# A Hyena and expert kernel: forward transform folded onto quarters of the array, with sends, stores and loads placed anew

## The chip, the core and the metric

The kernel runs on one core of one Trainium2 chip. The metric is the device time of one execution in microseconds (us). Names of engines: PE is TensorE's matmul, PEld its loading of weights, DVE VectorE, ACT ScalarE, POOL GpSimd, SP SyncE, which here only issues DMAs.

## The reference

The input is 4 batches of 11456 positions with 128 channels. The first half is a gated long convolution over each batch, by a filter that a small network and a window make; the second routes each of the 45824 rows to one of 8 experts.

```python
u = x * v
Uf, Hf = rfft(u, n=2*S, axis=1), rfft(h_filt, n=2*S, axis=0)
y = irfft(Uf * Hf, n=2*S, axis=1)[:, :S, :]
x = (x * y).reshape(B*S, D)
logits = x @ w_gate + modality_bias[modality_id]
e = argmax(logits); gate = softmax(logits)[e]
out[row] = gate * (relu(x[row] @ w1[e]) @ w2[e])
```

## The kernel before

**The convolution** is done as a transform in two factors (90 by 64) with matmuls in float32. It has, for each batch, an outer part and a middle part. The outer part goes over 16 steps q, each 8 channels: SP loads tiles of u and v (L446), DVE multiplies them (`product`, L451), and PE transforms the product (`forward`, L463; s in rows of the trace) with 64 matmuls of 128 rows by 90 columns that write halves of PSUM's partitions, two at a time; ACT copies the results into A (L466). The middle part goes over 23 groups g: ring loads of the filter's spectrum and two tables (h L579, b L576, c L584, into `rings`), a transform (pz, L595), the multiplication by the spectrum on DVE and POOL (L607 to L619), the transform back (pw, L638).

**The outer stage** from batch 1 on holds two things at once: the forward part of batch b, and the inverse part and routing of batch b - 1. In each step the inverse part turns two pieces of A (wt, L661), ACT copies them (L662), PE transforms them (py, L670), and y is made of the two halves of py: ACT copies one half (L673), DVE adds it to the other (L674) and subtracts it (L675), and multiplies the result by x, loaded at L655, into a row tile xo (L676). Two steps make a pair, of which the routing is done once: a turn of xo (xT, L705), the logits (pl, L716), their turn (lt, L725), the choice of expert (`shift`, `biased`, `choice`: L732 to L767, with an exponential on ACT, L753), the count of rows for each expert (pr, pn, L783 to L794, `send`). The rows go to memory (`store`, L774), and their places in the list of the chosen expert too (`places`, L801). The last outer stage has the inverse part and routing of batch 3 alone.

**Sends.** POOL scatters the rows to their expert's place (L268, one indirect DMA of 128 rows each) from tiles that are read back (L252). `send_rows(n)` puts n of them at a place in POOL's order. An outer step before has four: two behind the product, one behind y's sum, one behind the product with x. In the middle groups one or two follow `L619` from g = 5 on, and the experts issue one every third turn.

**The order** of the work is written by hand. Tables such as `OUTER` give each piece a step offset (`forward:2` is done for q in step q + 2), and within a step the order of the table stands; each engine takes its instructions in that order. `overlapped` and `early` mix the end of one stage with the start of the next by OV, EA, EM steps. Buffers named "a" (11 of 1024 float32 a partition) served x, u, v, y and the middle's parts in turn.

**The experts** take tiles of 512 or 256 rows. For a tile the rows are loaded (x, L991), turned (px, L1052) and split into two float32r parts (L1055, L1056), the weights too (w1r and w2r, L1006 and L1007; wl, L1041); PE forms the hidden layer (ph, L1069 to L1071) and the output (po, L1092 to L1094), which is scattered (L1111). `finale` holds the last pieces of routing, done beside the first tiles.

## Time and profile before

| | us |
|---|---|
| median of 3 runs | 2235.19 |
| lowest and highest | 2232.07, 2238.38 |
| profiled execution | 2249.8 |
| its span | 2248.0 |
| filter, then forward part of batch 0 | 0 to about 150 |
| outer stages of batches 1, 2, 3 | about 260 to 400, 515 to 655, 770 to 910 |
| middle stages of batches 1, 2 | about 400 to 513, 655 to 765 |
| last outer stage | about 1020 to 1115 |
| experts | about 1126 to 2248 |

How to read it: the profile's times are from one execution, recorded in the profiler. A row of a timeline or chain begins with its start in us from the start of the span, then its length in us. "L463" is line 463 of the kernel before. A bracket at the end tells how long the engine had been idle and what ended that.

### The profile page before, as it was taken

To read this page: it belongs to the slowest core of one execution; us is meant where nothing else is said; L and a number is where in the kernel's file an instruction comes from. 1 tells how busy PE (TensorE), PEld (TensorE's weight loads), DVE (VectorE), ACT (ScalarE), POOL (GpSimd) and SP (SyncE) were. 2 spreads that over 40 slices of the span, in tenths; PEclk is the share of its full clock that TensorE was granted. 3 is DMA by queue.
4 is the path that set the end of the run, shared out by engine and by line. 5 is a ranking of instruction groups with operands and counts; after the bars stand their busy time and mean duration, and the time that the engine had idled before them with its cause. 6 is when DMAs were issued, how large, how long until landed. Compare 5 with 4: busy or idle time off the path is not lost.

```text
span 2248.0 us, 49882 instructions
## 1 busy us (share of the span) xinstructions
PE 2160.9 (96%) x18746; PEld 1735.5 (77%) x18746; DVE 1668.0 (74%) x2847; ACT 1225.8 (55%) x2253; POOL 1025.1 (46%) x1032
## 2 busy tenths in 40 slices
PE   8989999899989999899799999999999999999996
PEld 8878777687768767676477888878888888888896
DVE  2348677995779767896877777767778877777796
ACT  4632366226642366225565666656666666666685
POOL 0116300695448754694335555545554333333332
PEclk9999999999999999999999999999999999999998
DMA  9576676777878788774657222222222111111111
GB/s 310 231 269 225 222 225 195 253 254 269 280 245 268 265 274 272 249 252 153 193 179 256 76 73 78 69 64 80 80 72 74 48 47 44 43 48 45 40 42 29
DMA packets 162526, 359.21 MB, mean 160 GB/s; under 512 B 25769, under 2 KB 59389, under 8 KB 162281
## 3 DMA queue, kind: packets, MB, share of 16 engines
q1 hardware_dynamic: 135625, 296.58, 41.0%
q0 software_dynamic: 26496, 59.36, 7.7%
q8 instruction: 150, 2.46, 0.4%
q14 instruction: 95, 0.78, 0.1%
q10 hardware_dynamic: 160, 0.03, 0.0%
HBM read 271.44 MB, written 84.83 MB: 158 GB/s over the span
## 4 chain that ended last, share of the span: by engine, by line
PE 55%; issue 26%; POOL 10%; DVE 4%; DMA 2%; ACT 2%; POOLq 0%; SPq 0%; ACTq 0%; DVEq 0%
PE pw L638 8%; PE s L463 7%; POOL out L1111 6%; PE pz L595 6%; PE py L670 5%; PE wt L661 5%; POOL xs L268 3%; PE po L1094 2%; PE xT L705 2%; PE ph L1069 2%; PE po L1092 2%; PE ph L1070 2%; PE ph L1071 2%; PE po L1093 2%; PE pl L716 1%
## 5 line engine op out<-in xcount | busy, mean ns | idle before, releaser
L1075 DVE SCALAR_TENSOR_TENSOR hl<-ph,hh 128x512 fp32r<-128x512 f32 x724 | 495.4, 689 | 220.8 <-ACT hh L1074 119.7
L1074 ACT ACTIVATE hh<-ph 128x512 fp32r<-128x512 f32 x724 | 433.7, 601 | 343.9 <-PE ph L1071 241.7
L1111 POOL DMA_INDIRECT out<-ot,idx x362 | 360.0, 994 | 556.1 <-DVE ot L1108 463.2
L268 POOL DMA_INDIRECT xs<-back,to x360 | 369.3, 1026 | 289.3 <-DVE y L674 103.8
L1069 PE MATMUL ph<-xh,wh 128*128 128x512 f32 (+1 forms) x792 | 306.3, 387 | 1.3 <-ACT xh L1055 1.3
L1092 PE MATMUL po<-hh,wh 128*128 128x512 f32 (+1 forms) x792 | 298.6, 377 | 4.0 <-issue 2.3
L1094 PE MATMUL po<-hl,wh 128*128 128x512 f32 (+1 forms) x792 | 297.1, 375 | 0.9 <-DVE hl L1075 0.7
L1070 PE MATMUL ph<-xh,wl 128*128 128x512 f32 (+1 forms) x792 | 297.1, 375 | 0.0
L1071 PE MATMUL ph<-xl,wh 128*128 128x512 f32 (+1 forms) x792 | 295.4, 373 | 0.0
L1093 PE MATMUL po<-hh,wl 128*128 128x512 f32 (+1 forms) x792 | 295.3, 373 | 0.0
L642 ACT COPY A<-pw 128x512 f32<-128x512 f32 (+1 forms) x184 | 97.7, 579 | 349.2 <-PE pw L638 339.9
L614 DVE TENSOR_TENSOR part<-pz,rings 128x1024 f32<-128x1024 f32 (+1 forms) x184 | 211.4, 1190 | 2.8 <-POOL part L619 2.8
L638 PEld LDWEIGHTS pw<-rings,part 64*128 64x128 f32 x2880 | 177.3, 189 | 35.6 <-issue 27.2
L638 PE MATMUL pw<-rings,part 64*128 64x128 f32 x2880 | 202.2, 279 | 1.7 <-POOL part L619 1.7
L595 PE MATMUL pz<-A,rings 128*64 128x256 f32 x1440 | 177.3, 388 | 13.8 <-DVE part L614 6.0
L609 POOL TENSOR_TENSOR more<-more 128x256 f32<-128x256 f32 (+1 forms) x92 | 73.9, 803 | 236.8 <-issue 150.0
L463 PE MATMUL s<-fwd,seq 128*64 128x90 f32 x4096 | 171.3, 242 | 9.5 <-issue 5.3
L1092 PEld LDWEIGHTS po<-hh,wh 128*128 128x128 f32 x792 | 149.2, 188 | 36.7 <-issue 4.4
L1094 PEld LDWEIGHTS po<-hl,wh 128*128 128x128 f32 x792 | 149.4, 189 | 35.5 <-DVE hl L1075 5.4
L463 PEld LDWEIGHTS s<-fwd,seq 128*64 128x64 f32 x4096 | 161.8, 137 | 18.6 <-issue 6.8
L1071 PEld LDWEIGHTS ph<-xl,wh 128*128 128x128 f32 x792 | 149.4, 189 | 29.7 <-DVE xl L1056 0.4
L1093 PEld LDWEIGHTS po<-hh,wl 128*128 128x128 f32 x792 | 149.3, 188 | 26.2
(184 smaller groups left out, 3705.2 us busy)
## 6 DMA issues: line engine op xcount, KB each, us to landing
rings<-hs SPq DMA_DIRECT2D x88, 512.0 KB
seq<-in_u SPq DMA_DIRECT2D x64, 512.0 KB
seq<-in_v SPq DMA_DIRECT2D x64, 512.0 KB
seq<-in_x SPq DMA_DIRECT2D x64, 512.0 KB
xr<-xo SPq DMA_DIRECT2D x64, 365.6 KB
back<-xr SPq DMA_DIRECT2D x72, 325.0 KB
rings<-in_c_b SPq DMA_DIRECT2D x88, 256.0 KB
rings<-in_c_c SPq DMA_DIRECT2D x88, 256.0 KB
```

What stands on the lines that cost most here:

```text
L268: s = pool.indirect_dma_start(out=xs, out_offset=bass.IndirectOffsetOnAxis(ap=ix, axis=0), in_=src, in_offset=None, bounds_check=E * R - 1 ...
L463: pe.matmul(v[64 * c:64 * c + 64, blk, j], u[:, blk, 4 * h + j], fwd[:, c], start=True, stop=True)
L638: pe.matmul(pw[par][:, to:to + D], t[at], k["c"][at, q, c], start=i == 0, stop=i == len(terms) - 1)
L1069: pe.matmul(p, k[0, "h"][:, f:f + D], k["xh"], start=True, stop=False)
L1070: pe.matmul(p, k[0, "l"][:, f:f + D], k["xh"], start=False, stop=False)
L1071: pe.matmul(p, k[0, "h"][:, f:f + D], k["xl"], start=False, stop=True)
L1074: act.activation(hh, ph, AF.Relu)
L1075: dve.scalar_tensor_tensor(hl, ph, 0.0, hh.bitcast(F32), op0=ALU.max, op1=ALU.subtract)
L1092: pe.matmul(po, k[1, "h"][:, f], hh[:, t], start=g == 0, stop=False)
L1093: pe.matmul(po, k[1, "l"][:, f], hh[:, t], start=False, stop=False)
L1094: pe.matmul(po, k[1, "h"][:, f], hl[:, t], start=False, stop=g == NCH - 1)
L1111: s = pool.indirect_dma_start(out=out, out_offset=bass.IndirectOffsetOnAxis(ap=k["idx"][:, j:j + 1], axis=0), in_=ot[:, j, :], in_offset=N ...
```

## The change

Forward parts of batches 1 to 3 are folded. The host reverses the order of one half of u and v, and the two halves of the product then come as a sum and a difference. DVE multiplies into a new tile p (109 partitions), POOL subtracts its halves and DVE adds them, into two slots of the ring `around`; the transform then has matmuls of at most 64 rows, in the order of four quarters (rows of the upper or lower half, columns of the left or right one). The number of matmuls is the same. Batch 0 keeps the old form.

y: ACT copies both halves of py (1024 elements) and DVE makes sum and difference of that copy a step later, in `combine`. Sends: one behind the product is gone, and the counts are 1 or 2 behind y's sum (turn about), 1 behind the product with x, 2.5 a step on the mean; in the middle stages they follow from the first group on for batches 2 and 3, and from g = 6 for batch 1; three every eight turns in the experts. Fetching rows back now goes by how many sends are left (`ready`). Stores come a step later; store and places of a batch's last step are issued in groups of the middle stage. The loads of x, u and v turn in 7 rows of `around`, p and y in 2 tiles, the middle's parts in 9. The ring's places differ, OV, EA and EM too. In the experts the results are three turns behind, in place of two, and the first tile's rows are loaded between w1r and w2r.

```diff
-OUTER = ("turn0:1 turn1:1 lturn:3 biased:3 forward:2 load_x:0 product:1 half:2 choice:3 "
-         "inverse:1 logits:2 send:4 shift:2 load:0 store:4 places:5")
-LAST = ("lturn:5 biased:5 send:6 turn0:1 choice:5 turn1:1 inverse:2 logits:4 half:3 shift:4 load_x:0 store:5 places:6")
+OUTER = ("turn0:1 turn1:1 biased:5 choice:5 send:6 forward:2 power:5 combine:2 gate:5 product:1 logits:4 half:3 "
+         "inverse:1 lturn:4 shift:4 load_x:0 load:0 store:6 places:6")
+LAST = ("lturn:5 biased:5 send:6 turn0:1 choice:5 power:5 gate:5 turn1:1 inverse:2 combine:2 logits:4 half:3 shift:4 "
+        "load_x:0 store:5")
...
-FIRST = "forward:17 load:0 product:16"
+FIRST = "forward:17 product:16 load:13"
...
-OV, EA, EM = 2, 3, 4
+OV, EA, EM = 4, 2, 5
...
-NA, NXO = 11, 3
+NA, NU, NS, NXO = 9, 7, 2, 3
...
-        for _ in range(min(n, len(waiting))):
+        for _ in range(n):
+            if ready and len(waiting) <= 2 * RC:
+                fetch(ready.pop(0))
+            if not waiting:
+                return
...
+        def next_a():
+
+            at = counts["around"] = (counts.get("around", -1) + 1) % NA
+            return around[:, at]
+
+        def rows_of(src, n=NU):
+
+            at = counts["rows", n] = (counts.get(("rows", n), -1) + 1) % n
+            t = around[:, at]
+            sp.dma_start(t, src)
+            return t
...
-            ("h", 2 * GW, (8 * GW, 0, 2 * GW)),
-            ("b", GW, (10 * GW, 4 * GW, 5 * GW)),
-            ("c", GW, (11 * GW, 6 * GW, 7 * GW)))}
+            ("h", 2 * GW, (8 * GW, 0, 4 * GW)),
+            ("b", GW, (10 * GW, 2 * GW, 6 * GW)),
+            ("c", GW, (11 * GW, 3 * GW, 7 * GW)))}
...
                 for name in ("u", "v"):
-                    t = kept[q, name] = new_a("seq")
-                    sp.dma_start(t, a[name][b, q])
+                    kept[q, name] = rows_of(a[name][b, q], NU if b else NA)
             def product(q):
-                u = kept[q, "u"]
-                s = dve.tensor_mul(u, u, kept.pop((q, "v")))
-                paced(s, 2)
+                if b == 0:
+                    of = kept[q, "of"] = kept.pop((q, "u"))
+                    dve.tensor_mul(of, of, kept.pop((q, "v")))
+                    return
+                u, v = kept.pop((q, "u"))[0:PU], kept.pop((q, "v"))[0:PU]
+                p, of = new_a("p")[0:PU], around[:, NU + q % (NA - NU)]
+                dve.tensor_mul(p, u, v)
+                pool.tensor_sub(of[0:PU, 512:1024], p[:, 0:512], p[:, 512:1024])
+                dve.tensor_add(of[0:PU, 0:512], p[:, 0:512], p[:, 512:1024])
+                kept[q, "of"] = of
             def transform(q):
-                u = kept.pop((q, "u")).rearrange("p (b d n) -> p b d n", b=2, n=N2)
+                of = kept.pop((q, "of")).rearrange("p (c d n) -> p c d n", c=2, n=N2)
+                whole = [(c, blk, slice(0, D), blk) for blk in range(2) for c in range(2)]
+                parts = [(c, blk, slice(64 * blk, 64 * blk + HALF), c)
+                         for c, blk in ((0, 0), (1, 1), (1, 0), (0, 1))]
                 for h in range(2):
                     p = pair("s1")
                     v = p[:, :, 0:4 * N1].rearrange("p b (d k) -> p b d k", d=4)
                     for j in range(4):
-                        for blk in range(2):
-                            for c in range(2):
-                                pe.matmul(v[64 * c:64 * c + 64, blk, j], u[:, blk, 4 * h + j],
-                                          fwd[:, c], start=True, stop=True)
+                        for c, blk, at, of_c in parts if b else whole:
+                            pe.matmul(v[64 * c:64 * c + 64, blk, j], of[at, of_c, 4 * h + j],
+                                      fwd[at, c], start=True, stop=True)
...
+                at = 3 * ((g + 1) % 3)
+                part = [around[:, at + i, 0:n * 4 * D].rearrange("p (c q b d) -> p c q b d", c=2, b=2, d=D)
+                        for i in range(2)]
+                more = around[:, at + 2, 0:n * 4 * D].rearrange("p (i c q d) -> p i c q d", i=2, c=2, d=D)
...
-                if g == 4 and b > 0:
-                    fetch(b - 1)
+                if g == 5 and b > 0:
+                    ready.append(b - 1)
...
-                if g > 4:
+                if g > 5 or b > 1:
...
-                t = kept[q] = new_a("seq")
-                sp.dma_start(t, a["x"][b, q])
+                if q == 0:
+                    counts.pop(("rows", NU), None)
+                kept[q] = rows_of(a["x"][b, q])
...
-                y = new_a("y")
-                act.copy(y[:, 512:1024], py[:, 1])
-                paced(dve.tensor_add(y[:, 0:512], py[:, 0], y[:, 512:1024]))
-                dve.tensor_sub(y[:, 512:1024], py[:, 0], y[:, 512:1024])
-                paced(dve.tensor_mul(xo_of(b, q // 2)[:, :, q % 2, :, 0:D], four(y),
-                                     four(kept.pop(q))))
-
-            return load, turn, transform
+                y = kept[q, "y"] = new_a("y")
+                act.copy(y, py.rearrange("p c m -> p (c m)"))
+
+            def combine(q):
+
+                y = kept.pop((q, "y"))
+                paced(dve.tensor_add(y[:, 0:512], y[:, 0:512], y[:, 512:1024]),
+                      1 + (q % 3 > 0 if b == nb - 1 else q % 2))
+                dve.scalar_tensor_tensor(y[:, 512:1024], y[:, 512:1024], -2.0, y[:, 0:512],
+                                         op0=ALU.mult, op1=ALU.add)
+                paced(dve.tensor_mul(xo_of(b, q // 2)[0:PU, :, q % 2, :, 0:D], four(y[0:PU]),
+                                     four(kept.pop(q)[0:PU])))
...
-                ex = powers[0:PU]
-                act.activation(ex[:, 0:E], dl, AF.Exp)
...
+            def power(o):
+                act.activation(powers[0:PU, 0:E], kept.pop(("dl", o)), AF.Exp)
+
+            def gate(o):
+                xo = xo_of(b, o)
                 se = rt.tile([PU, NC], F32, tag="se", name="se")
-                dve.tensor_reduce(se, ec(ex), axis=AX.X, op=ALU.add)
+                dve.tensor_reduce(se, ec(powers[0:PU]), axis=AX.X, op=ALU.add)
...
+                later.append([lambda f=todo[n]: f(NQ - 1) for n in ("store", "places")])
+                todo["store"] = but_last(todo["store"], 2)
+                todo.pop("places")
...
+                for k, g in enumerate(later.pop() if b else ()):
+                    mid[5 + k] = lambda f=mid[5 + k], g=g: (f(), g())
...
+    swap = lambda a: np.stack([a[0], a[1, :, ::-1]])
+    chan8 = lambda a: swap(a.reshape(2, 64, 2, N2, NQ, 8)).transpose(4, 0, 1, 2, 5, 3).reshape(NQ, D, -1)
```

In the experts:

```diff
-                sp.dma_start(k["w", 0], a["moe_w1"][ds(e, 1)].rearrange("e p f -> p (e f)"))
-                sp.dma_start(k["w", 1], a["moe_w2"][ds(e, 1)].rearrange("e (c p) d -> p (e c) d", p=D))
+                first = [lambda: sp.dma_start(k["w", 0], a["moe_w1"][ds(e, 1)].rearrange("e p f -> p (e f)")),
+                         lambda: sp.dma_start(k["w", 1], a["moe_w2"][ds(e, 1)].rearrange("e (c p) d -> p (e c) d", p=D))]
+                return first
+
+            of = raw_weights() if i < NDYN else []
+            for part in of[:1] + [rows] + of[1:] if i == 0 else [rows] + of:
+                part()
...
-            if lo == 0 and at >= FL + len(finale) + 2 and len(waiting) <= 2 * RC and not fetched:
-                fetched.append(fetch(nb - 1))
-            if lo == 0 and at % 3 == 0:
+            if lo == 0 and at == FL + len(finale) + 2:
+                ready.append(nb - 1)
+            if lo == 0 and 3 * at % 8 < 3:
...
-            result(at - 2)
-            if c == (5 if i <= last and tiles[i][2] == T else 2):
+            result(at - 3)
+            whole = i <= last and tiles[i][2] == T
+            if c == (4 if whole else 2):
                 rows_turn(i + 1)
+            if c == (5 if whole else 3):
                 rows_out(i - 1)
```

On DVE, these are the rows of an outer step from y's sums on, before (score, ix, lg, base are the routing's; seq holds u and v):

```order
L674 TENSOR_TENSOR y<-py,y 128x512
L675 TENSOR_TENSOR y<-py,y 128x512
L676 TENSOR_TENSOR xo_84<-y,seq 128x2x4x128
L790 TENSOR_TENSOR score<-pr,base 109x128
L791 TENSOR_TENSOR base<-base,pn 128x8
L792 TENSOR_TENSOR score<-score,oh_96 109x128
L794 TENSOR_REDUCE ix<-score 109x2x8
L732 TENSOR_TENSOR lg<-wf,bias 109x128
L732 TENSOR_TENSOR score<-wf,bias 109x128
L734 TENSOR_TENSOR lg<-lg,score 109x128
L741 TENSOR_TENSOR lg<-lt,lg 109x128
L451 TENSOR_TENSOR seq<-seq 128x1024
```

and after (around holds x, u, v and the folded product):

```order
L830 TENSOR_TENSOR score<-pr,base 109x128
L831 TENSOR_TENSOR base<-base,pn 128x8
L832 TENSOR_TENSOR score<-score,oh_95 109x128
L834 TENSOR_REDUCE ix<-score 109x2x8
L709 TENSOR_TENSOR y<-y 128x512
L711 SCALAR_TENSOR_TENSOR y<-y 128x512
L713 TENSOR_TENSOR xo_86<-y,around 109x2x4x128
L476 TENSOR_TENSOR p<-around 109x1024
L478 TENSOR_TENSOR around<-p 109x512
L769 TENSOR_TENSOR lg<-wf,bias 109x128
L769 TENSOR_TENSOR score<-wf,bias 109x128
L771 TENSOR_TENSOR lg<-lg,score 109x128
```

y's sums stand behind the row counts, both read y alone, and the product has the addition of its halves behind it.

On SP, where the outer stage of batch 1 ends and its middle stage begins (xr the stored rows, xi the places, rings the middle's loads), before:

```order
L774 DMA xr_58<-xo_85 90x1x1040 x2
L801 DMA xi_62<-ix 45x128 x2
L584 DMA rings<-in_c_c 128x512
L576 DMA rings<-in_c_b 128x512
L579 DMA rings<-hs 128x1024
```

and after:

```order
L814 DMA xr_58<-xo_84 90x1x1040 x2
L613 DMA rings<-in_c_c 128x512
L605 DMA rings<-in_c_b 128x512
L608 DMA rings<-hs 128x1024
...
L814 DMA xr_58<-xo_85 90x1x1040 x2
L613 DMA rings<-in_c_c 128x512
L605 DMA rings<-in_c_b 128x512
L608 DMA rings<-hs 128x1024
L841 DMA xi_62<-ix 45x128 x2
```

The last store and the places stood ahead of these ring loads, and now come behind three and four groups of them.

On SP, from the end of the last outer stage to the experts' first loads, before (TENSOR_LOAD reads a tile's expert and start):

```order
L774 DMA xr_61<-xo_86 90x1x1040 x2
L252 DMA back_92<-xr_60 128x650
L984 TENSOR_LOAD tab_100
L1002 TENSOR_LOAD tab_100
L1006 ISA
L1006 DMA w1r<-in_moe_w 128x1024
L1007 ISA
L1007 DMA w2r<-in_moe_w 128x8x128
L991 ISA
L991 DMA x<-xs 128x520
```

and after:

```order
L253 DMA back_92<-xr_60 128x650
L386 DMA around<-in_x 128x1024
L253 DMA back_90<-xr_60 128x650
L1034 TENSOR_LOAD tab_100
L1053 TENSOR_LOAD tab_100
L1057 ISA
L1057 DMA w1r<-in_moe_w 128x1024
L1042 ISA
L1042 DMA x<-xs 128x520
L1058 ISA
L1058 DMA w2r<-in_moe_w 128x8x128
```

The store is gone from there, and x stands between the two loads of weights.

## Rows read from the trace of the kernel before

**Rows 1.** The page's first part: busy time, share of the span, instructions of each engine.

```profile
PE 2160.9 (96%) x18746; PEld 1735.5 (77%) x18746; DVE 1668.0 (74%) x2847; ACT 1225.8 (55%) x2253; POOL 1025.1 (46%) x1032
```

**Rows 2.** Windows: stretch, length, busy PE, PEld, DVE, ACT, POOL, clock, DMA share, GB/s.

```profile
304.15:321.37 17.22, 17.01 (x210) 12.12 (x208) 12.10 (x26) 11.13 (x20) 0.00 (x0) 1.00 0.71 218
417.12:436.15 19.03, 19.01 (x256) 15.39 (x256) 18.66 (x23) 4.82 (x10) 14.94 (x15) 1.00 0.93 321
1800.00:2000.00 200.00, 200.00 (x938) 164.96 (x937) 154.26 (x252) 131.28 (x236) 67.33 (x68) 1.00 0.16 46
```

**Rows 3.** Chain of waits, outer stage of batch 1 and middle: start, length, instructions.

```profile
301.59 2.63 PE s L463 x64
304.22 0.90 PE xT L705 x8
305.12 1.87 PE py L670 x8
306.98 1.94 PE wt L661 x16
...
314.31 0.87 PE pl L716 x8
...
417.12 2.89 PE pw L638 x48
...
513.37 1.44 PE pw L638 x20
```

**Rows 4.** Timeline of DVE: start, length, instruction, idle before it.

```profile
306.12 0.40 DVE L764 TENSOR_REDUCE se<-powers 109x16 f32<-109x144 f32 x1 [0.17 <-ACT powers L753]
307.67 0.69 DVE L674 TENSOR_TENSOR y<-py,y 128x512 f32<-128x512 f32 x1 [0.83 <-ACT y L673]
310.26 1.22 DVE L451 TENSOR_TENSOR seq<-seq 128x1024 f32<-128x1024 f32 x1
314.98 0.69 DVE L674 TENSOR_TENSOR y<-py,y 128x512 f32<-128x512 f32 x1 [3.50 <-ACT y L673]
1122.43 0.29 DVE L734 TENSOR_TENSOR bs_late<-bs_late,score 109x128 f32<-109x128 f32 x1
```

**Rows 5.** Timelines of DVE and POOL in middle stages, where both work at once.

```profile
206.75 0.69 DVE L618 TENSOR_TENSOR part<-part 128x512 f32<-128x512 f32 x1
206.86 1.71 POOL L619 TENSOR_TENSOR part<-part 128x512 f32<-128x512 f32 x1 [0.84 <-DVE part L614]
741.79 1.27 DVE L618 TENSOR_TENSOR part<-part 128x512 f32<-128x512 f32 x1
741.76 0.74 POOL L609 TENSOR_TENSOR more<-more 128x256 f32<-128x256 f32 x1
743.61 1.27 POOL L619 TENSOR_TENSOR part<-part 128x512 f32<-128x512 f32 x1
```

**Rows 6.** Groups by line: count, busy, mean ns of one, idle before.

```profile
L673 ACT COPY y<-py 128x512 f32<-128x512 f32 x64 | 37.9, 592 | 61.3 <-PE py L670 49.2 <-issue 12.2
L268 POOL DMA_INDIRECT xs<-back,to x360 | 369.3, 1026 | 289.3 <-DVE y L674 103.8 <-issue 67.8 <-DVE mx L749 28.7
```

**Rows 7.** Timeline of PE: waits at the ends of stages.

```profile
415.17 1.95 PE L595 MATMUL pz<-A,rings 128*64 128x256 f32 x16 [2.02 <-DMA rings<-in_c_b]
1087.89 1.13 PE L661 MATMUL wt<-ident,A 128*90 128x128 f32 x8 [0.48 <-ACT rings L710]
1126.33 1.08 PE L1052 MATMUL px<-ident,x 128*128 128x128 f32 x4 [10.79 <-DMA x<-xs]
```

**Rows 8.** DMA issues on SP: start, length, transfer.

```profile
304.26 0.33 SPq L446 DMA_DIRECT2D seq<-in_u  x1
410.69 0.80 SPq L801 DMA_DIRECT2D xi<-ix  x2
412.05 0.37 SPq L576 DMA_DIRECT2D rings<-in_c_b  x1
1118.33 0.80 SPq L991 DMA_DIRECT2D x<-xs  x1
```

83 lines of the change are left out of this document (47 added, 36 removed).

## Prediction

> **What bounds the kernel now.** I read the views in the order in which a stage shows its limit: busy shares, windows by stage, the chain of waits inside one stage, then the timelines of the engines that wait. PE is busy for 96% of the span [rows 1]; that share is an average over unlike stages. The windows [rows 2] split it. In the outer stages, which run the inverse transform and routing of one batch beside the forward transform of the next, one pair of steps takes 17.22 us: PE is busy 17.01, DVE 12.10, ACT 11.13, DMA 71%. In the middle stages (four groups in 19.03 us) PE and DVE are both full, 19.01 and 18.66. In the experts PE is busy for all of 200 us. So PE is the limit nearly everywhere, and only in the outer stages has the next engine much room.
>
> The chain there [rows 3] is PE alone: the forward transform takes 2.63 us a step, the two turns 1.94, the inverse 1.87, the turn to the router 0.90 and once a pair the logits 0.87. DVE waits 3.50 and 0.83 us in the pair for ACT's copy, which waits for PE, and 0.17 more for the exponential [rows 4]. Its own work with issue gaps is so 17.22 - 4.50 = 12.72 us. That is what the change can reach: 3 outer stages (batches 1 to 3 forward) of 8 pairs, 24 pairs in all. Batch 0's forward part and the last outer stage have no folded transform.
>
> **The change part by part. PE.** Folding lets each matmul of the forward transform sum over 45 rows, inside a quarter of 64, where it summed over 128; the number of matmuls (64 a step) and their 90 columns stay, but four can stand in different quarters of the array, where two stood in its halves. The row on the forward transform gives 2.63/64/90 = 0.457 ns a column with two side by side; the logits put four side by side and take 0.87/8/436 = 0.25 ns [rows 3]. At 0.25 ns a step's 64 x 90 columns cost 1.44 us. A second floor is the loading of weights, one load of 64 columns before each matmul: 48 loads of 128 columns are hidden in 2.88 us [rows 3], 60 ns each, so a load of 64 columns needs at most 30 ns, and 64 of them 1.92 us. I keep 1.44 to 1.92 and, as the far end, the old 2.63. PE's pair falls from 17.01 by 2 x 0.71 to 1.19: 14.6 to 15.6 us.
>
> **DVE.** The product stays (1.22 us, row L451 of [rows 4]); the addition of its halves is new, 512 elements wide as the sum of y is, 0.69 us [rows 4]. y's two sums stay and read a copy from SBUF instead of PSUM; I take the same 0.69. So 12.72 + 2 x 0.69 = 14.1 us a pair. Then there is POOL's new subtraction, at the same moment as DVE's addition, since both wait for the product. An addition of this size took 0.69 us when it had begun before POOL's, and POOL's then took 1.71 instead of 1.27; it took 1.27 when it began inside POOL's subtraction [rows 5]. DVE lost 0.58 us there, and POOL 0.44 in the other order. Price per step: 0 at best; at worst what is left of POOL's operation after DVE's addition has ended, 206.86 + 1.71 - 207.44 = 1.13 us. I take 0.58, the one stretch of DVE shown: 2 x 0.58 = 1.2, DVE 15.3 us a pair (14.1 to 16.4).
>
> These prices rest on a rule too. The Trainium skill, "SBUF — State Buffer", section "Who interferes with whom", states that a VectorE operation with two inputs in SBUF and a GpSimd operation that reads SBUF share one port under an exclusive lock, and that the later one blocks fully. The rows agree: 741.76 + 0.74 + 0.69 = 743.19 us, and the addition ended at 743.06. It speaks against this change, for y's two sums now have both inputs in SBUF as well, where one came from PSUM; it is a rival below.
>
> **ACT, POOL, DMA.** ACT copies 1024 elements of y where it copied 512 (0.592 us [rows 6]), at most 0.59 more a step: 11.13 + 1.2 = 12.3 a pair, covered. POOL has 5 sends of 1.026 us a pair [rows 6] where it had 8, and two subtractions of 1.27 to 1.71: under 9 us, covered. The same bytes move in less time: 218 GB/s x 17.22/15.5 = 242, while a middle stage held 321 GB/s without a PE wait [rows 2]; covered.
>
> **The pair.** DVE at 15.3 and PE at 14.6 to 15.6 are close, and before the pair stood 0.21 above its PE (17.22 against 17.01). I add that to 15.3: 15.5 us. The outer term is 24 x (17.22 - 15.5) = -41 us.
>
> **The way into the middle stages.** PE waits 2.02 us for a ring load [rows 7], issued on SP at 412.05 behind the list of places (410.69, which waits for the routing) [rows 8]. The change issues that list after the loads, and starts the middle stage's transforms one turn earlier. The bounds are the whole of the PE wait plus as much again for the earlier start, -4, and 0; I take -3, three times: -9.
>
> **Sends in the middle stages.** Two of them get sends in five more groups, seven each, and one loses a group with sends. Four early groups, mostly without sends, take 19.03 us, 4.76 each [rows 2]; the 19 groups between the two chain rows at 417.12 and 513.37, most with sends, take 96.25/19 = 5.07 [rows 3]. 9 x 0.31 = +2.8; I take +3 (0 to +7, the latter with half of the 14 sends of 1.026 us on the path).
>
> **Last outer stage.** The wider copy of y stands on ACT ahead of the router's copies, for which PE waits 0.48 us [rows 7]. 16 steps x 0.59 = 9.4 if none is covered, 0 if all; half, +5.
>
> **Start of the experts.** PE waits 10.79 us for the first rows [rows 7], issued on SP at 1118.33 [rows 8] behind both weight loads and a store. The change puts them ahead of the second weights and takes the store away. But DVE's routing runs to 1122.72 [rows 4], and SP still waits for a transfer back. Bounds: the whole wait, -11, and +3 for three more pieces of routing behind the turn of the stages; I take -4. **Steady experts:** results three turns behind can't help a PE busy for 200.00 of 200 us: -1 (0 to -4). **Batch 0 and the filter:** later first loads, 0 (-2 to +5).
>
> The sum is -41 - 9 + 3 + 5 - 4 - 1 = -47. The profiled execution took 2249.8 us (span 2248.0), 15 above the median of 2235.19; the terms are differences, so I take them from the median: 2188.
>
> **The rivals.** (1) POOL's subtraction collides with nothing: DVE 14.1, PE 14.6 to 15.6. By PE's lower end the pair is 14.8, the outer term 24 x 2.4 = -58, the time 2171. For it: DVE's addition has no other engine's signal to wait for and starts first, as at 206.75 [rows 5]. (2) The full lock: every subtraction stops the next DVE operation for 1.13 us, DVE 16.4, the pair 16.6, the outer term -15, the time 2214. For it: y's sums and the routing's products now read SBUF twice. (3) The change doesn't do what it says: quarters in one row of the array share a path, the transform stays at 2.63, PE at 17.01. The outer term is 0 and the time 2229. Against it: the logits' 0.25 ns, though these share their rows and only differ in columns, which is why the case stays open.
>
> (4) **Slower: the loop of the loads.** Eleven buffers served x, u, v and y; now x, u and v turn in seven rows. In steady state the load of u waits for the row that y's last product (L713) has just read, and the product of the step after needs it. From L713 over the landing T, then that product and its sum (1.22 + 0.69), half of the routing's small work (12.10 less two steps of 1.22 + 0.69 + 0.69 + 1.22, halved: 2.2, some 2.6 with gaps) and the next y (0.69 + 0.69 + 1.22) to L713 two steps on: the pair is T + 7.1 us. It decides above T = 8.4 and loses from T = 10.1 on. The issue at 304.26 us served a product at 310.26, so T was at most 6.0 [rows 4, 8]; but sends and returning rows are added in two of the three stages. At T = 12 there the pair is 19.1: 16 x 1.9 = +30, the first stage -14, the rest -6: +10, 2245.
>
> The Trainium skill, "TensorE: Matmul & The Clock Gate", section "Wait — 56ns, not 53.3ns?", puts the start-to-start time of matmuls at no less than about 25 ns however small they are. The traced forward transform's 41 ns (2.63/64) neither confirms nor breaks it. By it a step's 64 matmuls would take 1.6 us, an estimate from that page, and rival 1 would come out at 2179 instead of 2171.
>
> **How the numbers follow.** My forecast with the collision of 0.58 us: 0.45 (its own range 2172 to 2204, from the pair at 15.1 to 15.9 and half of the small terms' bounds). Rival 1: 0.18. Rival 2: 0.17. Rival 3: 0.10. Rival 4: 0.10. The predicted time is the likeliest's, **2188**. The range reaches down past rival 1 with the outer-to-middle gain and the experts' start at better values, 2148, and up past rival 3, 2231; about 0.08 is left out below and 0.08 above. A measurement of this kernel can tell about 0.3% from no change, 6.7 us: 2228.5 to 2241.9. Faster: 0.45 + 0.18 + 0.17 and 0.04 of rival 3 = 0.84. The same: 0.05 of rival 3 and 0.03 of rival 4 = 0.08. Slower: 0.01 and 0.07 = 0.08.
>
> **What would show it.** In the profile after: the forward transform's row on the chain at 1.44 to 1.92 us (2.63: rival 3); the pair of steps in the second outer stage at 15.5 us, DVE busy above 90% of it and PE with waits for DVE; the new additions and y's first sum near 0.69 us where POOL is idle and near 1.27 where it subtracts (0.69 throughout: rival 1; DVE idle or stretched by over 1 us a step: rival 2); no wait of the product for a load (waits of over 2 us: rival 4). The PE wait for the ring load at the end of each outer stage should go, and the one for the first rows shrink by some 4 us. My prediction is wrong if DVE's idle time stays, that is if something other than PE's work ended its waits.

## The result and the profile after

The changed kernel takes 2253.28 us (median of 4 runs, 2249.24 to 2255.25), the kernel before 2234.28 (4 runs): a ratio of 1.0085, 95% interval 1.0072 to 1.0098. It is slower by 19 us where 2188 was forecast, and lies above the range.

The page of the changed kernel, its first part, answers [rows 1]:

```profile
span 2247.5 us, 49786 instructions
...
PE 2111.3 (94%) x18746; PEld 1690.8 (75%) x18746; DVE 1769.2 (79%) x2895; ACT 1249.4 (56%) x2253; POOL 1146.0 (51%) x1080
```

PE has 50 us less to do and DVE 101 more. The spans hardly differ, but the profiled execution of before was 15 us above its median. So stages are compared here, not spans.

Windows of the changed kernel: two pairs of outer steps of batch 1, then the end of that stage (the columns are those of [rows 2]).

```profile
315.73:331.98 16.25, 14.64 (x208) 9.70 (x208) 15.13 (x28) 11.52 (x20) 3.43 (x2) 1.00 0.70 240
331.98:349.64 17.66, 15.98 (x207) 10.74 (x207) 15.01 (x28) 11.51 (x20) 3.42 (x2) 0.90 0.64 220
400.00:412.00 12.00, 2.85 (x15) 1.64 (x17) 10.73 (x22) 1.38 (x3) 5.84 (x6) 0.66 0.56 189
```

PE's work in a pair fell as forecast, to 14.64 us, and DVE's rose to 15.1, but the pair takes 16.25 to 17.66 us, not 15.5. In the third window PE is idle for some 9 of 12 us.

PE's timeline there, with the forward transform of an earlier step first (answers [rows 3] and [rows 7]):

```profile
272.24 1.47 PE L492 MATMUL s<-fwd,around 45*64 45x90 f32 x64
273.64 0.96 PE L742 MATMUL xT<-ident,xo 109*128 109x109 f32 x8
...
397.04 2.95 PE L668 MATMUL pw<-rings,around 64*128 64x128 f32 x48
408.95 0.27 PE L823 MATMUL pr<-oh,both 109*128 109x128 bf16 x1 [8.96 <-DVE oh L794]
409.62 3.68 PE L624 MATMUL pz<-A,rings 128*64 128x256 f32 x16
...
725.47 3.68 PE L624 MATMUL pz<-A,rings 128*64 128x256 f32 x16 [5.78 <-DMA rings<-in_c_b]
729.08 4.06 PE L668 MATMUL pw<-rings,around 64*128 64x128 f32 x48
...
1131.92 0.63 PE L1114 MATMUL px<-ident,x 128*128 128x128 f32 x4 [1.39 <-DMA x<-xs]
```

and DVE's, ahead of the row count at 408.95 (L644 belongs to a middle group, L778 begins the choice):

```profile
403.48 2.34 DVE L644 TENSOR_TENSOR around<-pz,rings 128x1024 f32<-128x1024 f32 x2
...
406.47 0.28 DVE L778 TENSOR_TENSOR lg<-lt,lg 109x128 f32<-109x128 f32 x1
```

The transform takes 1.47 us for 2.63. The wait for the first rows of the experts fell from 10.79 us [rows 7] to 1.39. But the row count (pr) of an outer stage's last routing waits 8.96 us for DVE, and so in all three batches (8.96, 9.09, 9.09), where [rows 7] had 2.02 us for a ring load. In the middle stage of batch 2 there is a wait of 5.78 us, and the transform behind it takes 4.06 us for 2.95: the granted clock was at half there.

DVE and POOL in the two steps of a pair (answers [rows 5]), then DVE and PE in the experts' stage:

```profile
550.67 0.89 DVE L832 TENSOR_TENSOR score<-score,oh 109x128 f32<-109x128 f32 x1
...
555.77 0.73 DVE L478 TENSOR_TENSOR around<-p 109x512 f32<-109x512 f32 x1
556.43 1.85 DVE L769 TENSOR_TENSOR lg<-wf,bias 109x128 f32<-109x128 f32 x1
558.20 0.28 DVE L769 TENSOR_TENSOR score<-wf,bias 109x128 f32<-109x128 f32 x1
...
549.71 1.70 POOL L477 TENSOR_TENSOR around<-p 109x512 f32<-109x512 f32 x1 [0.67 <-PE wt L692]
...
555.78 0.98 POOL L273 DMA_INDIRECT xs<-back,to  x1 [0.30 <-DVE p L476]
556.77 1.36 POOL L477 TENSOR_TENSOR around<-p 109x512 f32<-109x512 f32 x1
...
1761.86 0.16 DVE L292 TENSOR_SCALAR fd<-nall 1x8 int32<-1x8 f32 x1 [10.99 <-SPq L989]
...
1763.69 0.79 PE L1154 MATMUL po<-hl,wh 128*128 128x512 f32 x1 [7.35 <-DVE hl L1135]
...
1768.55 0.63 PE L1153 MATMUL po<-hh,wl 128*128 128x512 f32 x1
...
1769.50 0.40 PE L1130 MATMUL ph<-xh,wl 128*128 128x512 f32 x1
```

The routing's first product (L769) lasts as long as POOL's subtraction goes on, 1.85 us for 0.28; in the other step L832 takes 0.89 for 0.28. In the experts DVE stands idle for 10.99 us ahead of a division of eight numbers, which waits for SP; PE waits 7.35 us behind it, and its matmuls run at the lower clock until 1769.1.

Measured from the first turn of one batch to that of the next, the three cycles took 253.3, 254.7 and 254.1 us before and 251.5, 265.3 and 253.0 after; from the last stage's first turn to the experts 102.0 and 101.8. Up to the experts, then, the loss stands in the cycle of batch 2 (10.6 us more); the other two gained 1 to 2 us, where the forecast's outer term alone is some 14 a cycle. Over all these, from the first turn to the experts, the granted clock was at its lower level (0.5) for 13 us before (9 of them in the wait just ahead of the experts) and for 85 after; a second trace of the changed kernel has 72.

### The profile page after: what moved, and what is told of

It reads as the page before. It is cut to its first block, busy times and chain, and to the rows that moved or that the text cites. A ratio compares the mean times of both kernels' runs of the same rounds, so it can differ in the third digit from the quotient of the medians.

```text
span 2247.5 us, 49786 instructions
## 1 busy us (share of the span) xinstructions
PE 2111.3 (94%) x18746; PEld 1690.8 (75%) x18746; DVE 1769.2 (79%) x2895; ACT 1249.4 (56%) x2253; POOL 1146.0 (51%) x1080
## 4 chain that ended last, share of the span: by engine, by line
PE 56%; issue 19%; DVE 9%; DMA 7%; POOL 6%; SPq 1%; ACT 1%; POOLq 0%; DVEq 0%; ACTq 0%
PE pw L668 10%; PE pz L624 7%; POOL out L1171 5%; PE ph L1131 4%; PE ph L1129 4%; PE ph L1130 4%; PE po L1152 4%; PE po L1154 4%; PE po L1153 4%; PE wt L692 3%; PE s L492 3%; PE py L701 3%; DMA xr<-xo 2%; DVE xo L713 2%; PE xT L742 1%
## 5 line engine op out<-in xcount | busy, mean ns | idle before, releaser
L1171 POOL DMA_INDIRECT out<-ot,idx x362 | 379.2, 1047 | 467.0 <-DVE ot L1168 382.4
L273 POOL DMA_INDIRECT xs<-back,to x360 | 398.8, 1108 | 264.6 <-DVE y L709 97.2
L1129 PE MATMUL ph<-xh,wh 128*128 128x512 f32 (+1 forms) x792 | 312.1, 394 | 0.7 <-ACT xh L1115 0.7
L668 PEld LDWEIGHTS pw<-rings,around 64*128 64x128 f32 x4320 | 250.5, 189 | 37.0 <-issue 30.3
L668 PE MATMUL pw<-rings,around 64*128 64x128 f32 x4320 | 267.3, 278 | 2.5 <-POOL around L649 2.4
L644 DVE TENSOR_TENSOR around<-pz,rings 128x1024 f32<-128x1024 f32 (+1 forms) x184 | 211.3, 1189 | 0.0
L624 PE MATMUL pz<-A,rings 128*64 128x256 f32 x1440 | 182.0, 397 | 8.6 <-DMA rings<-in_c_b 5.8
L1130 PEld LDWEIGHTS ph<-xh,wl 128*128 128x128 f32 x792 | 150.7, 190 | 24.5 <-DVE wl L1094 4.6
L1129 PEld LDWEIGHTS ph<-xh,wh 128*128 128x128 f32 x792 | 150.2, 190 | 20.5 <-ACT xh L1115 0.9
L492 PE MATMUL s<-fwd,around 45*64 45x90 f32 (+1 forms) x4096 | 127.7, 254 | 29.9 <-POOL around L477 12.3
```

The source lines that it names most:

```text
L273: s = pool.indirect_dma_start(out=xs, out_offset=bass.IndirectOffsetOnAxis(ap=ix, axis=0), in_=src, in_offset=None, bounds_check=E * R - 1 ...
L624: pe.matmul(pz[at, q, 2 * D * c:2 * D * c + 2 * D], k["b"][:, 2 * q + par, 64 * c:64 * c + 64], A[:, G * g + 2 * q + par].rearrange("p b d ...
L668: pe.matmul(pw[par][:, to:to + D], t[at], k["c"][at, q, c], start=i == 0, stop=i == len(terms) - 1)
L1129: pe.matmul(p, k[0, "h"][:, f:f + D], k["xh"], start=True, stop=False)
L1130: pe.matmul(p, k[0, "l"][:, f:f + D], k["xh"], start=False, stop=False)
L1171: s = pool.indirect_dma_start(out=out, out_offset=bass.IndirectOffsetOnAxis(ap=k["idx"][:, j:j + 1], axis=0), in_=ot[:, j, :], in_offset=N ...
```

## Experiments

Each ratio is against the kernel before on the same chip, with its 95% interval. The chips differ: the kernel before took 2235 to 2236 us beside the first and third series, and 2249 beside the second. The last three runs of the third series, which put one cause back each, were on another chip than the fastest variant, so they are compared by their ratios; by the intervals such a difference is good to some 5 us.

### First series: one suspect at a time, out of the changed kernel

**The subtraction on DVE.** POOL's subtraction, beside which DVE's operations are stretched, goes.

```diff
-pool.tensor_sub(of[0:PU, 512:1024], p[:, 0:512], p[:, 512:1024])
 dve.tensor_add(of[0:PU, 0:512], p[:, 0:512], p[:, 512:1024])
+dve.tensor_sub(of[0:PU, 512:1024], p[:, 0:512], p[:, 512:1024])
```

> One edit to the changed kernel: the difference of the product's halves is made by DVE behind the sum, not by POOL. In the changed kernel's trace a pair of outer steps takes 16.3 to 17 us where I forecast 15.5, the routing's first product (L769) takes 1.83 us instead of 0.28 and its last (L832) 0.84 instead of 0.28, each beside POOL's subtraction: 2.1 us a pair. Theory lock: that is what DVE loses, and DVE sets the pair. Then DVE gains 2.1 and pays 2 x 0.69: the pair falls by about 0.7 us, L769 and L832 are back at 0.28, and the time by 24 x 0.7 = 17, to about 2236. Rival (PE's lower clock and the ends of the stages hold the time, DVE's stretch is covered): pair and time stay within 5 us of 2253.

2254.65 us, 1.0079 (1.0052 to 1.0106): no change. The lock went (L832 0.28 us, L769 0.29), and PE's steps turned uneven, 11.7 and 6.5 us, 8.4 and 7.0: something else held them at some 16.8 us a pair. The timelines of SP and DVE in this variant:

```profile
338.42 0.33 SPq L386 DMA_DIRECT2D around<-in_u  x1
338.80 0.79 SPq L386 DMA_DIRECT2D around<-in_v  x1
339.63 1.75 SPq L814 DMA_DIRECT2D xr<-xo  x2
341.42 1.73 SPq L386 DMA_DIRECT2D around<-in_x  x1
...
337.17 1.23 DVE L713 TENSOR_TENSOR xo<-y,around 109x1024 f32<-109x1024 f32 x1
...
347.28 1.23 DVE L713 TENSOR_TENSOR xo<-y,around 109x1024 f32<-109x1024 f32 x1 [1.62 <-DMA around<-in_x]
```

The store of a tile xo goes out at 339.63, behind loads that wait for the product at 337.17; the next product, 10.1 us later, overwrites that very tile, one of three. The bracket names a load of x, but by the order of the loads the x that this product reads was issued two steps earlier, at 324.60, and the one at 341.42 serves a later product; what is left for it to wait for is the store.

**The overlap set back to 2 turns.**

```diff
-OV, EA, EM = 4, 2, 5
+OV, EA, EM = 2, 2, 5
```

> One number of the changed kernel set back: the middle stage overlaps the end of the outer stage by 2 turns, not 4. In the changed kernel's trace PE waits 9.0, 9.1 and 9.1 us at the ends of the three outer stages, its row count (pr, L823) behind DVE's last choice (L794), which stands behind two middle groups on DVE; each wait is followed by 10.2 us at a granted clock of 0.5. Theory order: with 2 turns only one group stands ahead of the choice, the wait falls to about 4.5, and the slow stretch behind it shrinks or goes: 3 x (4.5 + 0 to 5) = 14 to 28 us, 2225 to 2239. Rival (the wait is only another place for the end of the outer stage's routing, which must be done there anyhow): the middle stages come as much later as the wait gets shorter, 2253 within 5.

2255.2 us, 1.0084 (1.0061 to 1.0107): no change. The wait was split, 6.74 us in place of 9 and 1.45 at the row count before it, and the clock fell there as before.

**Half of the folded matmuls issued twice.**

```diff
-                        for c, blk, at, of_c in parts if b else whole:
+                        for c, blk, at, of_c in parts * (2 - h) if b else whole:
```

> The changed kernel with half of the folded transform's matmuls issued twice (the same values written again): PE has 0.72 us more a step, between the two kernels' loads, and nothing else moves. Theory clock: PE is not the limit in the outer stages any more, and what it idles there brings its granted clock down (0.97 over the span, 17 stretches at 0.5 between 330 and 1155 us, 96 us in sum, against 24 us before). With the added work the slow stretches in the outer stages shrink to under half, and the time stays or falls by up to 10 us, though PE does 24 x 2 x 0.72 = 35 us more. Rival (PE's work sets the pair and the clock follows from other things): the slow stretches stay, and the time grows by 15 to 35.

2259.99 us, 1.0102 (1.0078 to 1.0126). 35 us more work on PE cost 4 us by the ratios and 7 by the medians, so PE isn't what sets the outer steps. The stretches at the lower clock, from the first turn to the experts, took 85 us as in the changed kernel, and those inside the outer stages 31 for 37, not under half as the theory of the clock expected. But two traces of the changed kernel itself differ more (85 and 72 us, 37 and 24 inside the outer stages), so this run neither bears the theory out nor rules it out.

**The fold undone, all else kept.**

```diff
-                dve.tensor_mul(p, u, v)
-                pool.tensor_sub(of[0:PU, 512:1024], p[:, 0:512], p[:, 512:1024])
-                dve.tensor_add(of[0:PU, 0:512], p[:, 0:512], p[:, 512:1024])
+                dve.tensor_mul(of, kept.pop((q, "u")), kept.pop((q, "v")))
...
-                        for c, blk, at, of_c in parts if b else whole:
+                        for c, blk, at, of_c in whole:
```

> The changed kernel without the fold: batches 1 to 3 have the whole transform as batch 0 (128 rows, the old order of u and v, no sum and difference), all else of the change kept: y a step later, sends, stores, order of the stages, experts. It tells the fold from the rest. If the fold is a gain that other parts eat: PE is the limit again, a pair 17.2 us, the granted clock near 0.99 in the outer stages, and the time above the changed kernel's, by 24 x 0.5 = 12 us less what the clock gives back, 2255 to 2265. If the fold gains nothing or costs (lock and clock eat all of it): at or below 2253, and what is left above 2234 is the rest of the change, by my reading mainly 3 x 9 us of waits at the stages' ends and 9 us in the last outer stage.

2253.26 us, 1.0084 (1.006 to 1.0107), the time of the changed kernel. So the fold gained nothing in it, and the 19 us came from the rest. PE's pair took an even 16.4 us (7.8 and 8.6), less than the 17.2 before: the turn of A behind the logits (wt) takes 1.91 us where it took 2.76, probably with short waits inside. That y's work comes a step later is the likely reason; it was not tested by itself. The waits of 9 us at the ends of the stages, of 6.5 in the middle stage of batch 2 and of 7.4 at 1767 us are all there without the fold.

### Second series: the causes that the traces name, one by one and together

**An own buffer for the row counts.** SP reads eight counts from a small tile, each ahead of a transfer; the change let that tile share the buffer of the divisions.

```diff
-        end = new("fd", [1, E], I32)
+        end = new("end", [1, E], I32)
```

> One word of the changed kernel set back: the small tile end, from which SP reads eight row counts, has its own buffer again, and not that of the divisions (fd). In the changed kernel's trace DVE's next division (L292) waits 11.0 us for SP's last read (L989), since SP issues eight transfers in between; PE waits 7.35 us behind it (L1154, 1763.69) and its granted clock is 0.5 for 10.2 us after; the four variants run so far have the same slow stretch at 1773 to 1783. Theory: without the shared buffer the wait and the slow stretch go, 7.35 + 10.2/2 = 12 us, 2241. Rival (the read of the counts holds up DVE elsewhere, or the stretch is a chance stall as the one at 1477 us in the kernel before): 2253 within 4.

2269.57 us, 1.0084 (1.0055 to 1.0112), on a chip where this kernel's runs lay between 2263 and 2285: unclear, though the wait was gone from the trace. It was run again below.

**The store a step earlier.**

```diff
-         "inverse:1 lturn:4 shift:4 load_x:0 load:0 store:6 places:6")
+         "inverse:1 lturn:4 shift:4 load_x:0 load:0 store:5 places:6")
```

> One number of the changed kernel set back in spirit: the store of a pair's rows is issued in the step of its last entries, a step earlier. In the changed kernel the store of a tile xo (L814) comes just ahead of the product (L713) that overwrites the same tile, one of three: SP issues it after the loads of u and v, which wait for the step before, and the product waits until the rows have left. In the trace of the variant without POOL's subtraction a step so takes 10.1 us (338.4 to 348.5) and the next 6.9. Theory store: with the store a step earlier no product waits for it; the pairs of the outer stages fall from 16.3 to 17.6 us to what DVE does with the lock, about 16.3, even steps, and the time by 24 x 0.5 = 12, to 2241; with less PE idling fewer slow stretches. Rival (loads: the row of u, freed by the product, holds the step): pairs stay at 16.3 to 17.6 and the time within 5 of 2253.

2264.68 us, 1.0077 (1.0041 to 1.0113). Most of the uneven steps went in batch 1 (8.8 and 7.1 us), and POOL's lock was left: hardly a gain by itself.

**The last row count a turn later.**

```diff
-min(q + t, NQ + 4) if 0 < b < nb else q + t
+min(q + t, NQ + 5) if 0 < b < nb else q + t
...
-OV, EA, EM = 4, 2, 5
+OV, EA, EM = 5, 2, 6
```

> The last routing of an outer stage is moved against the middle groups: its row count on PE comes one turn later (behind one more group's matmuls), and DVE's last choice one group earlier (the cap of the last steps 5 in place of 4, overlap 5 and 6). In the changed kernel PE waits 9.0, 9.1 and 9.1 us for that choice and then runs 10.2 us at a granted clock of 0.5. Setting the overlap back alone (the variant with 2 turns) changed nothing: the wait was split, not removed. Theory order: here PE has matmuls to do until the choice is there, the wait falls under 3 us, and the slow stretch shrinks: 3 x (6 + 3) = 27 at most, 2226 to 2245. Rival (DVE is behind by that much at the end of the outer stage, whatever the order on PE): the wait comes back at the next group's matmuls (pz for DVE's parts), 2253 within 5.

2259.93 us, 1.0051 (1.0024 to 1.0077). The wait of 9 us fell apart into 1.8 and 2.5.

**All three, and the subtraction on DVE.**

> The three edits together (own buffer for the counts, store a step earlier, late row count), and the difference of the halves on DVE in place of POOL. If the three causes are separate, their gains add: 12 + 12 + 9 to 27, and with stores out of the way the lock is worth its 0.7 us a pair, 17: 2185 to 2205, faster than the kernel before, with pairs of 15.5 us and the granted clock under 1 in few stretches only. If PE's slower clock takes back what PE idles (a pair of 15.5 us has 12.9 of PE work), the pairs stay near 16.5 and the time comes to 2215 to 2235.

2229.78 us, 0.9898 (0.9859 to 0.9936): faster than the kernel before by 1.0%, and than any of the four alone by 1.5 to 1.9. They hide one another. It is less than the 0.978 to 0.987 that the single gains expected would have added up to.

### Third series: what each is worth

**The changed kernel and the own buffer again, on one chip.**

> The changed kernel itself again, on the same chip as the three runs beside it, since the chips differ (the kernel before took 2234 us on one and 2249 on another). Expected 1.0085 of the kernel before.

> The variant with the own buffer for the counts again, beside the changed kernel. Its first run was 1.0084 of the kernel before where I expected a gain of 12 us, though its trace has no wait at 1763 us any more. Theory buffer (the wait of 7.35 us and the slow stretch of 10.2 us behind it cost 12 us): 12 us under the changed kernel. Rival (the experts' stage gives the wait back elsewhere, for example in POOL's sends and scatters): the same as the changed kernel within 4 us.

2257.17 us, 1.010 (1.0081 to 1.0118), and 2244.30, 1.0041 (1.0027 to 1.0056): the buffer costs 13 us by these runs, 8 to 18 by their intervals. In the traces the experts' stage, from its first rows' turn to the end, takes 1115.5 and 1115.9 us with the shared buffer and 1108.0 without, 8 us. The first run was lost in the noise of its chip. The 12 us that both expectations work out are too much by some 2: of the 10.2 us at the lower clock (1758.8 to 1769.1) only the last 5.4 lie behind the wait, which ended at 1763.69.

**The fold undone in the variant with all edits.**

> The fold undone in the variant that was 1.0% faster than the kernel before: own buffer for the counts, store a step earlier and late row count are kept, the whole transform is back. It tells what the fold is worth when the other causes are out of the way. Theory fold: PE's pair is 16.4 us with the whole transform (measured in the variant without the fold) and 15.4 with the fold, so this one is 24 x 1.0 = 24 us above the folded one, 1.000 of the kernel before. Rival (PE's slower clock takes back what the fold gives): within 5 us of the folded one, 0.99.

2226.75 us, 0.9959 (0.9943 to 0.9975), against 0.9898 with the fold, on two chips: the fold is worth about 0.6% (0.2 to 1.0 by the intervals), 14 us, once DVE isn't held by other things. In the traces the three cycles take 754.3 us together without it and 743.9 with it.

**Rows fetched when 6 sends are left, not 10.** SP's timeline in the changed kernel (a list of places, loads of rows back, ring loads):

```profile
710.63 0.43 SPq L257 DMA_DIRECT2D to<-xi  x1
720.16 0.81 SPq L253 DMA_DIRECT2D back<-xr  x2
721.02 0.42 SPq L605 DMA_DIRECT2D rings<-in_c_b  x1
...
724.97 0.79 SPq L608 DMA_DIRECT2D rings<-hs  x1
733.21 0.33 SPq L613 DMA_DIRECT2D rings<-in_c_c  x1
```

Eight ring loads go out in one burst behind the load of rows back, which had waited 8.9 us for a send of POOL's to empty its buffer. PE's wait of 5.78 us ends with the first of them.

```diff
-            if ready and len(waiting) <= 2 * RC:
+            if ready and len(waiting) <= RC + 1:
```

> The variant that was 1.0% faster, with one number changed: the places of the next batch and its first rows are fetched when 6 sends are left, not 10. In all traces of the changed kernel and its variants SP waits some 9 us in the middle stage of batch 2 with a transfer of rows back into a buffer whose last send POOL has yet to do; the ring loads queue behind, PE waits 5.6 to 7.2 us (5.59 at 706.33 in this variant), and its granted clock is 0.5 for 6.8 us after. Theory queue: with 4 sends more in between, the buffer is free when SP comes to it, the PE wait goes: 5.6 + 3.4 = 9 us less, 0.986 of the kernel before. Rival (the rows then come too late for the sends, and POOL falls behind): the same or slower.

2195.46 us (2189.35 to 2196.71), 0.9820 (0.9804 to 0.9836): the fastest of all, 41 us under the kernel before; 0.986 was expected. The cycle of batch 2, where the burst stood, went from 257.7 to 240.3 us in the traces, the two others by 1 and 3 us. SP no longer stands there:

```profile
695.90 0.33 SPq L613 DMA_DIRECT2D rings<-in_c_c  x1
696.28 0.43 SPq L257 DMA_DIRECT2D to<-xi  x1
696.92 0.33 SPq L253 DMA_DIRECT2D back<-xr  x1
697.30 0.42 SPq L605 DMA_DIRECT2D rings<-in_c_b  x1
```

A pair of its outer steps (window, the columns as above):

```profile
321.00:336.30 15.30, 14.42 (x215) 9.65 (x211) 14.60 (x29) 11.57 (x20) 0.00 (x0) 1.00 0.76 265
```

15.3 us, with DVE busy for 14.6: what DVE has to do. Its cycles take 240.3, 240.3 and 241.8 us.

**One cause at a time, back into the fastest variant.** The subtraction on POOL:

> The fastest variant (0.982 of the kernel before) with one edit taken out: the difference of the halves is POOL's again. Its pairs of outer steps take 15.3 us with DVE busy 93%. Theory lock: POOL's subtraction stretches DVE's next operations by 2.1 us a pair, as in the changed kernel, while 2 x 0.69 of DVE's own work go: the pair grows by 0.7 to 16.0 us, the time by 24 x 0.7 = 17, to 0.990 of the kernel before. Rival (the lock was on the path only together with the late store): the pair falls to 14.6 by PE's work or stays, and the time is the same or up to 10 us less, 0.978 to 0.982.

2209.89 us, 0.9884 (0.9868 to 0.9901): 14 us for the lock. Pairs of 15.8 in batch 1, and of 16.1 to 16.4 on the mean in batches 2 and 3, where POOL has sends too (15.4 in all three in the fastest); groups by line of DVE, 300 to 370 us, in this variant and then in the fastest (count, busy, mean ns, idle):

```profile
L769 DVE TENSOR_TENSOR lg<-wf,bias 109x128 f32<-109x128 f32 x5 | 7.0, 1399 | 0.0
L832 DVE TENSOR_TENSOR score<-score,oh 109x128 f32<-109x128 f32 x4 | 3.6, 888 | 0.0
```

```profile
L769 DVE TENSOR_TENSOR lg<-wf,bias 109x128 f32<-109x128 f32 x5 | 1.4, 285 | 0.0
L832 DVE TENSOR_TENSOR score<-score,oh 109x128 f32<-109x128 f32 x4 | 1.1, 284 | 0.0
```

1.11 + 0.60 = 1.7 us a pair are lost in these two lines, and 2 x 0.69 of DVE's own work saved: 0.3 net in batch 1, and the forward transform waits for POOL besides. In batches 2 and 3 L769 takes up to 1.9 us.

The end of the stages as in the changed kernel:

> The fastest variant with the end of the outer stages as in the changed kernel (cap 4, overlap 4 and 5): PE's last row count stands ahead of the middle groups again. In the fastest variant PE waits 4.7 to 6.4 us there once a batch, for ring loads or DVE. Theory order: the wait of 9 us for the last choice is back in all three batches, with 10.2 us at a granted clock of 0.5 behind it: 3 x (9 - 5 + 3) = about 20 us, 0.991 of the kernel before. Rival (DVE's or the rings' lateness holds the end of the stage whatever PE's order): within 5 us, 0.982.

2211.27 us, 0.9886 (0.9869 to 0.9902): 15 us for the order. The wait of 9 us that was expected back is not there: the row count waits only 3.2 to 3.9 us, beside 5 to 7 us for ring loads, which the fastest variant has as well (4.7 and 5.0, and 6.4 for DVE in batch 3). The lower clock holds for 61 us from the first turn to the experts, against 34 in the fastest variant.

The store a step later, as in the changed kernel:

> The fastest variant with the store of a pair a step later, as in the changed kernel. Theory store: the product with x waits for the rows of the tile that it overwrites to have left, the steps turn uneven (10 and 7 us), the pair is 16.8 as in the variant without POOL's subtraction, 1.5 more: the time grows by 24 x 1.5 = 36 us, 0.998 of the kernel before. Rival (the loads of u, v and x held the step there, and the store only stood beside them): the pair stays at 15.3 to 15.6, under 8 us, 0.982 to 0.985.

2215.99 us, 0.9910 (0.9893 to 0.9926): 20 us for the store, where 36 was expected. DVE's products with x in this variant:

```profile
318.32 1.23 DVE L713 TENSOR_TENSOR xo<-y,around 109x1024 f32<-109x1024 f32 x1
...
327.84 1.23 DVE L713 TENSOR_TENSOR xo<-y,around 109x1024 f32<-109x1024 f32 x1 [1.03 <-DMA around<-in_x]
...
334.64 1.23 DVE L713 TENSOR_TENSOR xo<-y,around 109x1024 f32<-109x1024 f32 x1
...
344.78 1.24 DVE L713 TENSOR_TENSOR xo<-y,around 109x1024 f32<-109x1024 f32 x1 [1.66 <-DMA xr<-xo]
```

Steps of 9.5, 6.8 and 10.1 us; in the fastest variant no such wait stands. The store itself is named here.

## Why the prediction was wrong

**PE's transform: right.** 1.47 us, at the lower end of 1.44 to 1.92; rival 3 (no overlap of quarters) is out.

**DVE becomes the limit of the pair: right, and its sum too.** The working gave 12.72 + 2 x 0.69 for the additions, and the fastest variant adds 2 x 0.69 for the subtraction: 15.5, measured 15.3. PE's and DVE's busy time stand in the window as forecast, and DVE's idle time in a pair fell from 5.1 us to 1.1 and 2.7 in the changed kernel, 0.7 in the fastest variant. What is left in the changed kernel is waits that the forecast did not have.

**The lock: mis-sized.** I took 0.58 us a step, from the one stretch of DVE in [rows 5]. It is 1.57 and 0.61 in the two steps at 550 to 558 us, 2.2 a pair, which is the far end of the bounds, 2 x 1.13; rival 2 was right. I took the stretch of an operation that begins inside POOL's; in one step here POOL, held by a send, begins only after DVE's addition, and the next operation with two inputs in SBUF (L769) lasts until POOL has ended (558.28 and 558.13 us). In the fastest variant it costs 14 us. The rule of the Trainium skill ("SBUF — State Buffer", "Who interferes with whom") was the better guide: the later one blocked fully. The trace agrees with these two ends.

**The late store: a term that the sum didn't have.** The change part tells what the diff does to loads, sends and the list of places; the store a step later has no price in it at all. It was to be found in the order: the store of a tile stands on SP behind two loads that wait for one product, and the very next product overwrites that tile. 20 us by the last run. Rival 4 had the same queue, and named the wrong buffer: the product of u and v waited 0.4 us for its loads in 82 us of the changed kernel (300 to 382), the product with x, which overwrites the tile, 3.7.

**The way into the middle stages: the wrong sign.** I forecast -9 from the ring load and SP's order. The new overlap put DVE's last choice behind two middle groups, and PE's row count ahead of its next group: 9 us of wait, three times. I had the order of SP for this place, and not that of PE and DVE. 15 us by the run, in which the wait is 3.2 to 3.9 us: the rest of the 9 stood only together with the other causes. Nor did the waits for ring loads go for good, as the forecast had it: with the order mended, they are back at 4.7 and 5.0 us in the fastest variant.

**Fetching rows by sends left: no term either.** `ready` stands in the diff; priced were the sends on POOL, which cost next to nothing (the fastest variant's cycles with and without sends in the early groups: 240.3 and 240.3, forecast +3). What cost was SP, standing in order behind POOL: 0.9898 to 0.9820, some 17 us with what followed (8 to 27 by the intervals), and 17.4 in the cycle of batch 2 alone.

**The experts: the steady part was forecast at -1, and a shared small buffer cost 8 to 13.** The buffer is one word of the diff. The stage took 1121.7 us before, with a stray stop at about 1477 us and 6.8 us of lower clock behind it, and 1108.0 with the own buffer, so the steady part seems to have gained several us more than forecast; there is one trace of the kernel before, and I have not taken it apart. At the start, the forecast +5 for the last stage and -4 for the experts' start came out at -0.2 together (102.0 to 101.8); PE's wait for the rows went, and a new one for DVE's part of the weights came, 4.24 us at 1137.97.

**The sum of what was missed.** 14 + 20 + 15 + 17 + 13 = 79 us by single runs; with all away the time falls by 62 (1.010 to 0.982). They overlap, probably since the lock, the store and the order lie on the same engine's queue. The forecast's own kernel, with the subtraction on POOL and the four unpriced causes away, is the variant at 0.9884: -26 us, where I forecast -47 and rival 2's full lock gives -21. So what I priced was too good by the lock, and what I left unpriced made a loss of the rest. That the fastest variant's -41 is close to -47 is luck in part: it has the subtraction on DVE, which the forecast did not have, it lacks the -9 at the stages' ends, and the experts seem to have given more than their -5.

**The granted clock.** Not in the forecast. From the first turn to the experts it was at the lower level for 85 us (72 in the second trace), in stretches that begin within waits of PE or shortly behind one, and for 34 in the fastest variant, which has the same work for PE. The long ones outlast the wait: PE stood from 399.99 to 408.95 us with the lower clock from 403.8 to 414.0, and from 1756.3 to 1763.69 with it from 1758.8 to 1769.1. In what is left behind the wait, some 5 us, PE's work takes nearly twice its time (3.68 us for 1.95 in the pz at 409.62, a matmul every 0.43 us for 0.23 in the experts). So such a wait costs its length and some 2.5 us more, 10 us for the shared buffer's 7.35 as an estimate from these rows. The expectations, which set the whole 10.2 us behind the wait, had too much. Whether filling PE would keep the clock up was tried in one way (twice the matmuls), with no clear answer; it stays open.

## What to carry to other kernels

Price every line of a diff, above all those that move a store, a fetch or a small buffer: here the transform and DVE's additions came out as worked out, and five small things, worth 13 to 20 us each by single runs, one mis-sized and four without a price, turned a gain into a loss. For each tile that is written again, look up in the order what must have left it, and how many instructions lie between; for each in-order queue, ask which engine its head now waits for. Waits on one engine hide each other: take out one alone and little moves, so put them back one by one into a version without any.

## What was not expected of the hardware

Four quarters of the array, taken in the order of the diagonal first, started 64 matmuls of 45 rows by 90 columns in 1.40 us (272.24 to 273.64), 21.9 ns from one to the next. The Trainium skill, "TensorE: Matmul & The Clock Gate", section "Wait — 56ns, not 53.3ns?", gives about 25 ns as the least; the measurement is under it, so this is no floor with the matmuls in different quarters.

A wait of PE costs more than its length: in the 7.35 us ahead of 1763.69 the clock fell, and it stayed at the lower level for 5.4 us behind them, with a matmul every 0.43 us for 0.23, so that the place cost some 10 us (an estimate from these rows).
